# Attention and feed-forward in one kernel: two token blocks share each weight group, and the last tokens' value remainders take 128 rows

## The chip, the cores and the metric

The kernel runs on one core of one Trainium2 chip. The metric is the device time of one execution in microseconds (us); lower is better. Engines: PE (TensorE: matmuls; its weight loads are shown as PEld), DVE (VectorE), ACT (ScalarE), POOL (GpSimd) and SP (SyncE, which issues the DMAs here). All run side by side, and each takes its own instructions strictly in the order in which they stand in its program.

## The reference

Linear attention over 8 batches, 8 heads and 576 tokens of 64 values, then a feed-forward layer (512 to 2048 to 512) over the 4608 tokens, all in float32:

```
def phi(x):                                   # x: b h s 64, w_phi: 64 x 128
    proj = einsum('bhsd,df->bhsf', x, w_phi)
    proj = proj - max(abs(proj), axis=-1)
    return concatenate([exp(proj), exp(-proj)], axis=-1)
q_p, k_p = phi(q), phi(k)
kv  = einsum('bhsf,bhsd->bhfd', k_p, v)
den = einsum('bhsf,bhf->bhs', q_p, sum(k_p, axis=2))[..., None] + 1e-6
x   = (einsum('bhsf,bhfd->bhsd', q_p, kv) / den)     # tokens x 512
h   = x @ w_in
out = maximum(0.01 * h, h) @ w_out
```

## The kernel before

**Attention** works on 32 *pairs* (a batch and two of its heads; four pairs make a batch). `k_phase(i)` turns the keys and values of pair i into a 256 x 66 matrix; `q_phase(i)` projects the queries (L317 for pairs 4 to 7, L319 and L320 later), transposes, subtracts the maximum, transposes back into `mb` (L338), takes the exponentials, multiplies with the pair's matrix (L358), divides (L369 to L374) and leaves x in `ring`. `ring` has two halves, one for even and one for odd batches. Pairs 0 to 3 go a quicker way at the start: `first_k_phase`, and `first_q_phase` in three units of 256, 256 and 64 tokens, so that unit 0 makes the x of token block 0 and unit 1 that of block 1. Pairs below 8 (`nat`) use plain float32 matmuls; from pair 8 on each operand is split in a rounded part and a remainder (names ending in h and l), and the product takes three matmuls.

**The feed-forward layer** works on 18 blocks of 256 tokens and 16 groups of 128 hidden values. One *step* (i, ft) is `layer1` (12 matmuls of 256 columns into the PSUM tile `h`, then `g` on ACT, `gh` on ACT, `gl` on POOL) and `layer2` (6 matmuls of 512 columns into two PSUM tiles `acc`). `split(i)` cuts a block's x in `xh` and `xl`. The blocks come one after the other.

**The weights** arrive in 32 *pieces* (`load_weights`: w_in and w_out for each of the 16 groups), as 64-bit words that are turned into float32 on the chip: two ACT operations, four DVE operations (L158, L159, L160, L163), a cast on ACT and a remainder on DVE (L72, `w0l` or `w1l`). The raw words of all pieces go through two places in the odd half of `ring` (`stage`). So no x of batch 1 can be written there until the last piece has been read.

**What sets the order**: the program is written with priorities (weights and attention ahead of the feed-forward steps), and a scheduler lays every instruction into its engine's fixed order at build time. `advance` and `room` say how far attention may run ahead. PSUM has eight banks: three `a` (attention's projections), one `c`, two `h`, two `acc`. Tiles with one tag share its buffers: a tile waits until an earlier holder of its buffer has been read for the last time.

**The last 64 tokens** of a pair (512 to 575) are kept for both heads in one tile, `kst`: rows 64 to 127 hold the rounded part, rows 0 to 63 the remainder. Their value remainders `vl` stand in rows 64 to 127 alone, so that the product L266 runs over 64 rows; L267, beside it, runs over 128.

Of the kernel before, what the change touches and what calls it, by code (L numbers as in the profile page):

```python
# [44 lines left out]
def attention_moe_kernel(ctx: ExitStack, tc: tile.TileContext, q, k, v, vt, w_phi, w_in, w_out, out):  # L45
# [5 lines left out]
    def ct(shape, dt, name):  # L51
        return cp.tile(shape, dt, tag=name, name=name)
# [39 lines left out]
    wq = ct([P, 2, F], F32R, "wq")  # L92
    wq_h, wq_l = wq[:, 0], wq[:, 1]
    bd = ct([P, 2 * F], F32, "bd")
    vh = ct([P, 10, 66], F32R, "vh")
    vl = ct([P, 10, 64], F32R, "vl")
    nc.gpsimd.memset(vh[:, :, 64:66].bitcast(F32), 1.0)

    f1, f2, f3, f4 = (cp.tile([P, 2048], F32, tag="late", name=n, bufs=4) for n in ("f1", "f2", "f3", "f4"))
    fk = [None, f2, f1, f4]  # L100
# [41 lines left out]
            nc.scalar.copy(wq_h[r], w)  # L142
            nc.vector.tensor_tensor(wq_l[r], w, wq_h[r].bitcast(F32), op=ALU.subtract)

    stage = ring[:, 1].rearrange("p a s -> p (a s)")

    def load_weights():
        n = 0
        for ft in range(NFT):
            for which, src in ((0, w_in), (1, w_out)):  # L150
                raw = stage[:, 1024 * (n % 2) : 1024 * (n % 2) + 1024].bitcast(I32)
                nc.sync.dma_start(raw, src[:, ft].bitcast(I32))
                raw = raw.rearrange("p (n t) -> p n t", t=2)
                low, top = raw[:, :, 0], raw[:, :, 1]
                w = st([P, DM], F32, "ql")
                wi = w.bitcast(I32)
                nc.scalar.activation(w, top.bitcast(F32), AF.Abs)
# [21 lines left out]
        kraw[i] = rk, rv  # L179

    def load_q(i):
        rq = st([P, S], F32, "qs" if i < NN and i % 2 else "rq")
        nc.sync.dma_start(rq, q[i])
        qraw[i] = rq

# [2 lines left out]
    def k_phase(i):  # L188
        nat = i < NK
        rk, rv = kraw.pop(i)  # L190
        if not nat:
            ks = st([P, 2, S], F32R, "ks")
            for j in range(2):
                o, n = slice(64 * j, 64 * j + 64), slice(64 - 64 * j, 128 - 64 * j)
                copy_("kh", ks[o, j], rk[o])
                nc.vector.tensor_tensor(ks[n, j], rk[o], ks[o, j].bitcast(F32), op=ALU.subtract)
            copy_("vh", vh[:, :, 0:64], rv[:, :, 0:64])
            for r, c in ((slice(0, P), slice(0, 8)), (slice(64, P), slice(8, 10))):
                tt_("vl", vl[r, c], rv[r, c, 0:64], vh[r, c, 0:64].bitcast(F32), ALU.subtract)
# [9 lines left out]
        for g in range(3):  # L209
            w = 2 if g < 2 else 1  # L210
            r = slice(0, P) if g < 2 else slice(64, P)
            n = P if g < 2 else 64
            m4 = st([P, 4], F32, "m4")
            pmk = st([P, 4, F], F32, "pmk")
            if nat:
                pk = pt("a")
                for s in range(w):
                    t0 = (2 * g + s) * P if g < 2 else S - P
                    proj(pk, s, rk[:, t0 : t0 + P])
                pkv = pk[r, 0 : 256 * w].rearrange("p (a f) -> p a f", f=F)  # L220
            else:
                for s in range(w):
                    t0 = (2 * g + s) * P if g < 2 else S - P
                    pk = pt("a")
                    for j in range(2):
                        nc.tensor.matmul(pk[:, 256 * j : 256 * j + 256], lhsT=ks[:, j, t0 : t0 + P],
                                         rhs=wq.rearrange("p a f -> p (a f)"), start=True, stop=True)
# [12 lines left out]
            yield  # L240
            for s in range(w):
                c = 2 * g + s
                ek = st([P, 2, 256], F32, ("ek", "kph", "kpl")[c % 3] if nat else "ek")
                nc.scalar.activation(ek[r, :, 0:F], pmk[r, 2 * s : 2 * s + 2], AF.Exp)  # L244
                nc.scalar.activation(ek[r, :, F:256], pmk[r, 2 * s : 2 * s + 2], AF.Exp, scale=-1.0)
                if nat:
                    for j in range(2):
                        kv_mm(j, rv[r, 4 * j + c if c < 4 else 8 + j], ek[r, j], first=c == 0, last=c == 4)
                    yield
                    continue  # L250
                if c < 4:
                    kph = st([P, 2, 256], F32R, "kph")
                    kpl = st([P, 2, 256], F32R, "kpl")
                    copy_("kph", kph, ek)
                    tt_("kpl", kpl, ek, kph.bitcast(F32), ALU.subtract)
                    for j in range(2):
                        kv_mm(j, vh[:, 4 * j + c], kph[:, j], first=c == 0)
                        kv_mm(j, vl[:, 4 * j + c], kph[:, j])
                    for j in range(2):
                        kv_mm(j, vh[:, 4 * j + c], kpl[:, j])  # L260
                else:
                    kst = st([P, 2, 256], F32R, "kph")
                    copy_("kst", kst[r], ek[r])
                    nc.vector.tensor_tensor(kst[0:64], ek[r], kst[r].bitcast(F32), op=ALU.subtract)
                    for j in range(2):
                        kv_mm(j, vl[r, 8 + j], kst[r, j])  # L266
                        kv_mm(j, vh[:, 8 + j], kst[:, j], last=True)  # L267
                yield
        kvs = st([P, 2, 256], F32, "ek").rearrange("p a (b f) -> p a b f", b=2)[0:66]
# [254 lines left out]
    accs = {}  # L524
    gs = {}

    def split(i):
        for d in range(NP):
            t0 = 0
            while t0 < T:  # L530
                c = (i * T + t0) % (2 * S)
                n = min(T - t0, S - c % S)
                x = ring[:, c // S, d, c % S : c % S + n]
                t1 = t0 + n
                copy_("xh", xh[:, d, t0:t1], x)
                tt_("xl", xl[:, d, t0:t1], x, xh[:, d, t0:t1].bitcast(F32), ALU.subtract)
                t0 = t1

    def layer1(i, ft):
        ph = pt("h")[:, 0:T]  # L540
        for d in range(NP):
            nc.tensor.matmul(ph, lhsT=weight(0, "h", ft)[:, d * P : d * P + P], rhs=xh[:, d], start=d == 0, stop=False)  # L542
            nc.tensor.matmul(ph, lhsT=weight(0, "l", ft)[:, d * P : d * P + P], rhs=xh[:, d], start=False, stop=False)  # L543
        for d in range(NP):
            nc.tensor.matmul(ph, lhsT=weight(0, "h", ft)[:, d * P : d * P + P], rhs=xl[:, d], start=False, stop=d == NP - 1)  # L545
        g = st([P, T], F32, "g")
        gh = st([P, T], F32R, "gh")
        gl = st([P, T], F32R, "gl")
# [34 lines left out]
    def room(i):  # L583
        return min(B, 2 + i * T // S) * NP
# [3 lines left out]
    together(first_k_phase(0), first_k_phase(1))  # L588
    together(first_k_phase(2), first_k_phase(3))
    together(first_q_phase(0))  # L590
    tc.cur_priority = PU
    first_load_q(1)
    first_load_q(2)
    together(first_q_phase(1))
    together(first_q_phase(2))
    split_w_phi()
    load_q(NP)
    tc.cur_priority = PW
    load_weights()
    tc.cur_priority = 0  # L600
    steps = [(i, ft) for i in range(NBLK) for ft in range(NFT)]
    split(0)
    for n, (i, ft) in enumerate(steps):
        layer1(i, ft)
        advance(min(room(i + 1), NP * (1 + (i + (ft + 1) / NFT) * T / S) + 2))
        if ft == NFT - 1 and i + 1 < NBLK:
            advance(math.ceil((i + 2) * T / S) * NP)
            split(i + 1)
        if n >= LAG:
            layer2(*steps[n - LAG])  # L610
# [39 lines left out]
```

## Time and profile before

| | |
|---|---|
| median of 3 runs | 1243.11 us (1240.61 to 1243.74) |
| the profiled execution | 1238.5 us, its span 1236.7 us |
| PE busy | 1187.8 us, 96% of the span |
| DVE, ACT, POOL busy | 854.6, 797.0, 669.4 us |
| mean granted TensorE clock | 0.994 |
| DMA | 57.00 MB, mean 46 GB/s |

A row of the timeline gives the start in us from the span's start, the duration, the engine, the line, and what is written and read. A row of the windows gives, for a stretch, each engine's busy time with the number of its instructions. PE's busy time can hide waiting, since matmuls overlap and their ends are modelled; the distance from one matmul's start to the next, and the number of matmuls in a stretch, tell more. A float32 matmul is recorded as two instructions.

### The profile page before, as it was taken

To read this page: it belongs to the slowest core of one execution; us is meant where nothing else is said; L and a number is where in the kernel's file an instruction comes from. 1 tells how busy PE (TensorE), PEld (TensorE's weight loads), DVE (VectorE), ACT (ScalarE), POOL (GpSimd) and SP (SyncE) were. 2 spreads that over 40 slices of the span, in tenths; PEclk is the share of its full clock that TensorE was granted. 3 is DMA by queue.
4 is the path that set the end of the run, shared out by engine and by line. 5 is a ranking of instruction groups with operands and counts; after the bars stand their busy time and mean duration, and the time that the engine had idled before them with its cause. 6 is when DMAs were issued, how large, how long until landed. Compare 5 with 4: busy or idle time off the path is not lost. (4 is left out here: it accounts for less than half of the span.)

```text
span 1236.7 us, 21143 instructions
## 1 busy us (share of the span) xinstructions
PE 1187.8 (96%) x7496; PEld 1035.8 (84%) x7496; DVE 854.6 (69%) x1357; ACT 797.0 (64%) x2027; POOL 669.4 (54%) x701
## 2 busy tenths in 40 slices
PE   8898799999999999999899999999999999999998
PEld 5686577779888989889798988989888888999997
DVE  6999854698888888888888898806887788200000
ACT  5987765677777777777677777736766766433232
POOL 0132122467767676767667777836666767433232
PEclk9999899999999999999999999999999999999999
DMA  7345411011111111111111111100111100000000
GB/s 209 116 135 160 147 47 41 10 54 34 39 30 48 31 35 44 31 48 31 30 38 39 31 48 31 39 20 28 31 48 31 29 20 1 19 17 1 18 18 17
DMA packets 62777, 57.00 MB, mean 46 GB/s; under 512 B 45136, under 2 KB 46288, under 8 KB 62672
## 3 DMA queue, kind: packets, MB, share of 16 engines
q1 hardware_dynamic: 62672, 55.65, 15.8%
q8 instruction: 59, 0.97, 0.3%
q14 instruction: 46, 0.38, 0.1%
HBM read 46.20 MB, written 9.44 MB: 45 GB/s over the span
## 5 line engine op out<-in xcount | busy, mean ns | idle before, releaser
L72 POOL TENSOR_TENSOR gl<-g,gh 128x256 fp32r<-128x256 f32 x288 | 241.9, 842 | 294.8 <-ACT gh L67 237.1
L542 PE MATMUL h<-xh,w0h 128*128 128x256 f32 x1152 | 299.1, 286 | 4.5 <-ACT g L549 1.8
L543 PE MATMUL h<-xh,w0l 128*128 128x256 f32 x1152 | 298.2, 285 | 0.4 <-DVE w0l L72 0.4
L562 PE MATMUL acc<-w1h,gh 128*128 128x512 f32 x576 | 231.0, 401 | 10.4 <-ACT gh L67 8.3
L542 PEld LDWEIGHTS h<-xh,w0h 128*128 128x128 f32 x1152 | 218.4, 190 | 21.2 <-ACT g L549 2.7
L543 PEld LDWEIGHTS h<-xh,w0l 128*128 128x128 f32 x1152 | 218.2, 189 | 14.3 <-issue 1.9
L563 PE MATMUL acc<-w1l,gh 128*128 128x512 f32 x576 | 228.5, 397 | 0.0
L564 PE MATMUL acc<-w1h,gl 128*128 128x512 f32 x576 | 220.3, 398 | 0.0
L545 PE MATMUL h<-xl,w0h 128*128 128x256 f32 x1152 | 206.3, 284 | 0.0
L549 ACT ACTIVATE g<-h 128x256 f32<-128x256 f32 x288 | 109.2, 382 | 133.3 <-PE h L545 93.6
L72 POOL TENSOR_TENSOR ql<-eq,qh 128x576 fp32r<-128x576 f32 x96 | 159.5, 1668 | 38.7 <-DVE qh L69 26.3
L545 PEld LDWEIGHTS h<-xl,w0h 128*128 128x128 f32 x1152 | 167.2, 190 | 2.1 <-issue 0.4
L67 ACT CAST gh<-g 128x256 fp32r<-128x256 f32 x288 | 114.3, 402 | 75.5 <-PE acc L563 72.3
L562 PEld LDWEIGHTS acc<-w1h,gh 128*128 128x128 f32 x576 | 109.0, 189 | 26.3 <-ACT gh L67 10.5
L72 POOL TENSOR_TENSOR kpl<-ek,kph 128x512 fp32r<-128x512 f32 x72 | 101.9, 1415 | 49.9 <-PE c L206 22.1
L69 DVE CAST qh<-eq 128x576 fp32r<-128x576 f32 x96 | 99.2, 1037 | 35.5 <-ACT eq L344 20.1
L564 PEld LDWEIGHTS acc<-w1h,gl 128*128 128x128 f32 x576 | 106.6, 189 | 19.5 <-POOL gl L72 0.5
L563 PEld LDWEIGHTS acc<-w1l,gh 128*128 128x128 f32 x576 | 109.1, 189 | 12.4
L69 DVE COPY o<-acc 128x512 f32<-128x512 f32 x17 | 11.7, 687 | 130.4 <-DMA out_dram<-o 129.5
L72 POOL TENSOR_TENSOR ring<-ring,mb 128x576 f32<-128x576 f32 (+1 forms) x37 | 47.9, 1293 | 88.2 <-DVE mb L500 42.9
L343 ACT ACTIVATE eq<-mb 128x288 f32<-128x288 f32 x112 | 49.3, 440 | 67.8 <-DVE mb L338 60.4
L244 ACT ACTIVATE ek<-pmk 128x256 f32<-128x256 f32 (+1 forms) x128 | 53.4, 417 | 58.6 <-POOL pmk L72 21.0
(176 smaller groups left out, 2412.3 us busy)
## 6 DMA issues: line engine op xcount, KB each, us to landing
out_dram<-o SPq DMA_DIRECT2D x35, 256.0 KB, 2.0
ring<-in_w_in_dram SPq DMA_DIRECT2D x16, 512.0 KB, 3.7
ring<-in_w_out_dram SPq DMA_DIRECT2D x16, 512.0 KB, 3.6
rk<-in_k_dram SPq DMA_DIRECT2D x27, 288.0 KB, 2.8
rq<-in_q_dram SPq DMA_DIRECT2D x26, 288.0 KB, 2.8
rv<-in_v_dram SPq DMA_DIRECT2D x29, 256.0 KB, 3.4
rv<-in_vt_dram SPq DMA_DIRECT2D x58, 32.0 KB, 2.9
f<-in_k_dram SPq DMA_DIRECT2D x3, 288.0 KB, 3.3
```

Source lines behind the costliest of these rows:

```text
L67: nc.scalar.copy(o, i)
L69: (nc.vector if e == "v" else nc.gpsimd).tensor_copy(o, i)
L72: (nc.vector if pick(key) == "v" else nc.gpsimd).tensor_tensor(o, a, b, op=op)
L244: nc.scalar.activation(ek[r, :, 0:F], pmk[r, 2 * s : 2 * s + 2], AF.Exp)
L343: nc.scalar.activation(eq[:, 0], mb[:, u], AF.Exp)
L542: nc.tensor.matmul(ph, lhsT=weight(0, "h", ft)[:, d * P : d * P + P], rhs=xh[:, d], start=d == 0, stop=False)
L543: nc.tensor.matmul(ph, lhsT=weight(0, "l", ft)[:, d * P : d * P + P], rhs=xh[:, d], start=False, stop=False)
L545: nc.tensor.matmul(ph, lhsT=weight(0, "h", ft)[:, d * P : d * P + P], rhs=xl[:, d], start=False, stop=d == NP - 1)
L549: nc.scalar.activation(g, ph, AF.Prelu, alpha=0.01)
L562: nc.tensor.matmul(a, lhsT=gh[:, ts], rhs=weight(1, "h", ft), start=ft == 0, stop=False)
L563: nc.tensor.matmul(a, lhsT=gh[:, ts], rhs=weight(1, "l", ft), start=False, stop=False)
L564: nc.tensor.matmul(a, lhsT=gl[:, ts], rhs=weight(1, "h", ft), start=False, stop=ft == NFT - 1)
```

## The change

1. **Blocks 0 and 1 take each weight group together.** The first 32 steps are (0,0), (1,0), (0,1), (1,1) and so on; block 1's x is split right after `first_q_phase(1)`. Its rounded part sits in the two buffers of `qh` (which pairs from 8 on need), its remainder in a tile `vx`, which is handed to the value tile `vhl` (the former `vh` and `vl`) once block 1 is through layer 1. Block 1's two output sums take one bank of `h` and one of `a`, so that one `h` and two `a` are left until both blocks are done.
2. **Raw words go elsewhere.** Pieces 0 to 9 go through the odd half of `ring`, 10 to 23 through the tiles `f4` and `f1` of the quick start (the second half of `f4` holds the matrix of pair 2 until unit 2 of the first queries has used it), and 24 to 31 through the second half of `ring`'s odd half (the places of pairs 6 and 7) and a buffer of `qs`. So x of pairs 4 and 5 may be written from piece 10 on, and x of pairs 6 and 7 after piece 30. The queries of pairs 5 and 7 no longer have a buffer of their own.
3. **128 rows.** Rows 0 to 63 of the last tokens' value remainders are set to zero once, and their product runs over all 128 rows. It now also waits for the remainder that DVE writes into rows 0 to 63 of `kst`.

```
+    xbh = [st([P, 2, U], F32R, "qh")[:, :, 0:T] for _ in range(2)]
+    xbl = cp.tile([P, NP, T], F32R, tag="vx", name="xbl", bufs=1)
...
+    def values():
+        if not split_v:
+            split_v[0] = vhl = cp.tile([P, 10, 130], F32R, tag="vx", name="vhl", bufs=1)
+            nc.gpsimd.memset(vhl[:, :, 64:66].bitcast(F32), 1.0)
+            nc.gpsimd.memset(vhl[0:64, 8:10, 66:130].bitcast(F32), 0.0)
+        return split_v[0][:, :, 0:66], split_v[0][:, :, 66:130]
...
-                raw = stage[:, 1024 * (n % 2) : 1024 * (n % 2) + 1024].bitcast(I32)
+                if n < 10:
+                    raw = ring[:, 1, 2 * (n % 2) : 2 * (n % 2) + 2].rearrange("p a s -> p (a s)")[:, 0:1024]
+                elif n < 24:
+                    raw = (f4[:, 0:1024], f4[:, 1024:2048], f1[:, 0:1024])[n % 3]
+                else:
+                    raw = st([P, 2 * S], F32, "qs")[:, 0:1024] if n % 2 else tail_stage[:, 0:1024]
...
-        rq = st([P, S], F32, "qs" if i < NN and i % 2 else "rq")
+        rq = st([P, S], F32, "rq")
...
-                        kv_mm(j, vl[r, 8 + j], kst[r, j])
+                        kv_mm(j, vl[:, 8 + j], kst[:, j])
...
+    split(0)
...
+    split(1, *xb)
...
+    for t in range(TT):
+        accs[1, t] = pt(('h', 'a')[t])
+        nc.vector.memset(accs[1, t][:, 0:1], 0.0)
+        accs[0, t] = pt("acc")
...
-    steps = [(i, ft) for i in range(NBLK) for ft in range(NFT)]
-    split(0)
+    steps = [(i, ft) for ft in range(NFT) for i in range(2)]
+    steps += [(i, ft) for i in range(2, NBLK) for ft in range(NFT)]
     for n, (i, ft) in enumerate(steps):
-        layer1(i, ft)
-        advance(min(room(i + 1), NP * (1 + (i + (ft + 1) / NFT) * T / S) + 2))
-        if ft == NFT - 1 and i + 1 < NBLK:
+        if i == 1:
+            layer1(i, ft, *xb)
+        else:
+            layer1(i, ft)
+        advance(min(room(0 if n < 2 * NFT - 1 else i + 1), NP * (1 + (n + 1) / NFT * T / S) + 2))
+        if i and ft == NFT - 1 and i + 1 < NBLK:
```

Three places show how the instructions move; the line numbers are those of each kernel's own file (the changed file's L396, L508, L562, L563, L565 and L582 to L584 are L378, L490, L542, L543, L545 and L562 to L564 before; its L175 to L180 are L158 to L163, its L335 is L317 and its L376 is L358). On PE, this is the last pair of unit 1 of the first queries (`c<-qs`) and unit 2 behind it (`128x64`), with the steps around them. Before:

```order
L490 MATMUL c<-qs,f_79 128x256 x2
L564 MATMUL acc<-w1h_718,gl 128x512 x2
L542 MATMUL h<-xh,w0h_705 128x256
L317 MATMUL a<-rq,bd 128x288
L543 MATMUL h<-xh,w0l_706 128x256
```

Steps of block 0 alone surround it. After:

```order
L508 MATMUL c<-qs,f_82 128x256 x2
L396 MATMUL a<-bd,ks 128x256 x2
L562 MATMUL h<-qh,w0h_638 128x256
L563 MATMUL h<-qh,w0l_639 128x256
L508 MATMUL c<-eq,f_81 128x64 x2
```

Before, block 0's steps with later groups (`w0h_705` is the second tile of four groups) stand around them; now it is the first step of block 1 (`qh` is its x), which needs the x of all four pairs, and the next step of block 0 stands behind it.

On DVE, this is where piece 10 of the weights (its L158, now L175) comes. Before, pieces go on all the while between the divisions of the first queries (L497 to L500):

```order
L500 STREAM_TRANSPOSE mb<-rc 128x256
L158 TENSOR_SCALAR ql<-ql 128x512
L163 ISA ql<-ql,kvl 128x1024
L234 TENSOR_REDUCE m_1007<-a 128x4
L159 TENSOR_SCALAR ql<-ql 128x512
```

Pieces and attention take turns there. After, all of the first queries and the keys of pair 4 and some of pair 5 stand ahead of it:

```order
L517 RECIPROCAL rc<-mb 128x8
L518 STREAM_TRANSPOSE mb<-rc 128x256
L255 TENSOR_TENSOR pmk<-a,m_1062 64x256
L175 TENSOR_SCALAR ql<-ql 128x512
L176 TENSOR_SCALAR ql<-ql 128x512
L177 SCALAR_TENSOR_TENSOR ql<-f_83,ql 128x512
```

Piece 10 (read from `f_83`, which is `f4`) now stands behind the last division of unit 2.

On PE again, this is where pair 6 multiplies with its matrix (`a<-eq,kvh`). Before, it stands in block 1, in the third group of weight tiles:

```order
L564 MATMUL acc<-w1h_718,gl 128x512
L542 MATMUL h<-xh,w0h_797 128x256
L358 MATMUL a<-eq,kvh 128x288 x2
L543 MATMUL h<-xh,w0l_798 128x256
L358 MATMUL a<-eq,kvh 128x288
```

They are woven one by one into a layer 1. After:

```order
L584 MATMUL a<-w1h_835,gl 128x512
L376 MATMUL a<-eq,kvh 128x288 x4
L294 MATMUL c<-ident,ek 128x66 x4
L562 MATMUL h<-qh,w0h_914 128x256
L563 MATMUL h<-qh,w0l_915 128x256
```

It stands in the fourth group (`w0h_914`) between steps of block 0 and block 1, and PE can take none of the rows behind it until its exponentials are there.

More of the change, by code (lines that the diff above doesn't have):

```diff
@@ L94, in attention_moe_kernel @@
     bd = ct([P, 2 * F], F32, "bd")
-    vh = ct([P, 10, 66], F32R, "vh")
-    vl = ct([P, 10, 64], F32R, "vl")
-    nc.gpsimd.memset(vh[:, :, 64:66].bitcast(F32), 1.0)
+    xbh = [st([P, 2, U], F32R, "qh")[:, :, 0:T] for _ in range(2)]
+    xbl = cp.tile([P, NP, T], F32R, tag="vx", name="xbl", bufs=1)
+    for x in xbh:
+        nc.gpsimd.memset(x[:, 0, 0:2].bitcast(F32), 0.0)
+    nc.gpsimd.memset(xbl[:, 0, 0:2].bitcast(F32), 0.0)
+    xb = [xbh[d // 2][:, d % 2] for d in range(NP)], [xbl[:, d] for d in range(NP)]
+    split_v = {}
+    def values():
[4 more added lines that the diff above has]
+        return split_v[0][:, :, 0:66], split_v[0][:, :, 66:130]
     f1, f2, f3, f4 = (cp.tile([P, 2048], F32, tag="late", name=n, bufs=4) for n in ("f1", "f2", "f3", "f4"))
@@ L143, in split_w_phi @@
             nc.vector.tensor_tensor(wq_l[r], w, wq_h[r].bitcast(F32), op=ALU.subtract)
-    stage = ring[:, 1].rearrange("p a s -> p (a s)")
+    tail_stage = ring[:, 1, 2:4].rearrange("p a s -> p (a s)")
     def load_weights():
@@ L150, in load_weights @@
             for which, src in ((0, w_in), (1, w_out)):
-                raw = stage[:, 1024 * (n % 2) : 1024 * (n % 2) + 1024].bitcast(I32)
+                if n < 10:
[4 more added lines that the diff above has]
+                    raw = st([P, 2 * S], F32, "qs")[:, 0:1024] if n % 2 else tail_stage[:, 0:1024]
+                raw = raw.bitcast(I32)
                 nc.sync.dma_start(raw, src[:, ft].bitcast(I32))
@@ L196, in k_phase @@
                 nc.vector.tensor_tensor(ks[n, j], rk[o], ks[o, j].bitcast(F32), op=ALU.subtract)
+            vh, vl = values()
             copy_("vh", vh[:, :, 0:64], rv[:, :, 0:64])
@@ L525, in attention_moe_kernel, with split @@
     gs = {}
-    def split(i):
+    x0 = [xh[:, d] for d in range(NP)], [xl[:, d] for d in range(NP)]
+    def split(i, xh=x0[0], xl=x0[1]):
         for d in range(NP):
@@ L534, in split, with layer1 @@
                 t1 = t0 + n
-                copy_("xh", xh[:, d, t0:t1], x)
-                tt_("xl", xl[:, d, t0:t1], x, xh[:, d, t0:t1].bitcast(F32), ALU.subtract)
+                copy_("xh", xh[d][:, t0:t1], x)
+                tt_("xl", xl[d][:, t0:t1], x, xh[d][:, t0:t1].bitcast(F32), ALU.subtract)
                 t0 = t1
-    def layer1(i, ft):
+    def layer1(i, ft, xh=x0[0], xl=x0[1]):
         ph = pt("h")[:, 0:T]
         for d in range(NP):
-            nc.tensor.matmul(ph, lhsT=weight(0, "h", ft)[:, d * P : d * P + P], rhs=xh[:, d], start=d == 0, stop=False)
-            nc.tensor.matmul(ph, lhsT=weight(0, "l", ft)[:, d * P : d * P + P], rhs=xh[:, d], start=False, stop=False)
+            nc.tensor.matmul(ph, lhsT=weight(0, "h", ft)[:, d * P : d * P + P], rhs=xh[d], start=d == 0, stop=False)
+            nc.tensor.matmul(ph, lhsT=weight(0, "l", ft)[:, d * P : d * P + P], rhs=xh[d], start=False, stop=False)
         for d in range(NP):
-            nc.tensor.matmul(ph, lhsT=weight(0, "h", ft)[:, d * P : d * P + P], rhs=xl[:, d], start=False, stop=d == NP - 1)
+            nc.tensor.matmul(ph, lhsT=weight(0, "h", ft)[:, d * P : d * P + P], rhs=xl[d], start=False, stop=d == NP - 1)
         g = st([P, T], F32, "g")
```

## The prediction

> **What bounds the kernel now.** I read the page's first lines, then the windows, then the timelines of PE and DVE over the first 260 us, and at last the groups by shape.
>
> ```profile
> span 1236.7 us, 21143 instructions
> ...
> PE 1187.8 (96%) x7496; PEld 1035.8 (84%) x7496; DVE 854.6 (69%) x1357; ACT 797.0 (64%) x2027; POOL 669.4 (54%) x701
> ```
>
> PE is the bound over the whole; the next engine is at 69%. Where PE falls short is read from the windows (busy us and number of instructions of each engine):
>
> ```profile
> 0.00:60.00 60.00, 51.48 (x235) 36.41 (x236) 47.62 (x92) 44.19 (x93) 4.66 (x17) 1.00 0.58 166
> 60.00:100.00 40.00, 37.47 (x216) 31.72 (x215) 38.26 (x73) 33.29 (x75) 12.44 (x15) 1.00 0.47 141
> 100.00:160.00 60.00, 48.57 (x233) 35.25 (x232) 52.11 (x96) 43.96 (x96) 8.42 (x12) 0.91 0.46 135
> 160.00:240.00 80.00, 80.00 (x449) 63.91 (x448) 44.14 (x83) 46.83 (x128) 29.05 (x38) 1.00 0.14 38
> 240.00:260.00 20.00, 16.33 (x82) 12.38 (x81) 15.18 (x31) 15.42 (x37) 6.49 (x10) 0.91 0.26 73
> 260.00:1060.00 800.00, 781.39 (x5204) 700.67 (x5203) 652.01 (x980) 557.11 (x1452) 550.88 (x533) 1.00 0.12 33
> 1060.00:1220.00 160.00, 160.00 (x1019) 144.83 (x1018) 4.61 (x7) 52.66 (x140) 53.78 (x76) 1.00 0.03 12
> ```
>
> From 1060 on there is no attention left and PE runs dense: 1019 matmuls in 160 us. In 100 to 160 it starts 233 in 60 us, in 240 to 260 it starts 82 in 20 us; DVE is busy 90.4 of the 100 us from 60 to 160 (38.26 + 52.11), then 44 of 80. So PE starves in the first 160 us, where DVE has the weights and attention together, and once more at 240. Afterwards it is nearly full.
>
> These rows of the timelines place four events: the last piece of the weights on DVE, pair 6's first transpose into `mb`, pair 7's last query projection on PE, and the first matmul of block 2 that waited for the x of pair 7.
>
> ```profile
> 161.70 0.67 DVE L72 TENSOR_TENSOR w1l<-ql,w1h 128x512 fp32r<-128x512 f32 x1
> ...
> 203.94 0.77 DVE L338 STREAM_TRANSPOSE mb<-tq 128x576 f32<-128x576 f32 x1
> ...
> 226.94 0.75 PE L317 MATMUL a<-qs,bd 64*128 64x288 f32 x2
> ...
> 255.09 0.39 PE L542 MATMUL h<-xh,w0h 128*128 128x256 f32 x1 [0.65 <-ACT xh L67]
> ```
>
> **Part 3 of the change, the 64-row matmuls.** The groups by shape, and two of these matmuls among their neighbours:
>
> ```profile
> L206 PE MATMUL c<-kph,vl 128*64 128x256 f32 x192 | 49.5, 280 | 0.0
> L206 PE MATMUL c<-kph,vl 64*64 64x256 f32 x48 | 15.7, 328 | 0.7 <-DVE kph L69 0.7
> L206 PEld LDWEIGHTS c<-kph,vl 128*64 128x64 f32 x192 | 25.8, 134 | 2.2
> L206 PEld LDWEIGHTS c<-kph,vl 64*64 64x64 f32 x48 | 6.2, 129 | 10.4 <-issue 5.4 <-DVE kph L69 1.6 <-DVE kph L264 0.6
> ```
>
> ```profile
> L264 DVE TENSOR_TENSOR kph<-ek,kph 64x512 fp32r<-64x512 f32 x24 | 18.9, 786 | 0.8
> ```
>
> ```profile
> 280.49 0.40 PE L564 MATMUL acc<-w1h,gl 128*128 128x512 f32 x1
> 280.73 0.28 PE L542 MATMUL h<-xh,w0h 128*128 128x256 f32 x1
> 280.84 0.28 PE L543 MATMUL h<-xh,w0l 128*128 128x256 f32 x1
> 281.05 0.33 PE L206 MATMUL c<-kph,vl 64*64 64x256 f32 x1
> 281.31 0.39 PE L542 MATMUL h<-xh,w0h 128*128 128x256 f32 x1
> 281.53 0.28 PE L543 MATMUL h<-xh,w0l 128*128 128x256 f32 x1
> 281.65 0.28 PE L542 MATMUL h<-xh,w0h 128*128 128x256 f32 x1
> ...
> 282.00 0.27 PE L206 MATMUL c<-kph,vh 128*66 128x256 f32 x1
> 282.20 0.33 PE L206 MATMUL c<-kph,vl 64*64 64x256 f32 x1
> 282.46 0.34 PE L206 MATMUL c<-kph,vh 128*66 128x256 f32 x1
> 282.63 0.40 PE L226 MATMUL a<-wq,ks 128*128 128x256 f32 x2
> ```
>
> A 256-column matmul normally starts 0.12 us after the one ahead (280.73 to 280.84, 281.53 to 281.65), and a 512-column one takes 0.23 (280.49 to 280.73 for 0.24). Around the 64-row one three distances are long: to it 0.21, from it 0.26, and from the next 0.22. That is 0.69 instead of 0.36, a loss of 0.33 us; at 282.20 it is 0.20, 0.26 and 0.17, a loss of 0.27. The weight load's idle time says the same: 10.4 us ahead of 48 loads of 64 rows, 2.2 ahead of 192 loads of 128 rows. PE evidently neither overlaps the load of a 64-row operand with the matmul ahead nor the next load with it. With 128 rows the matmul has the shape of the 192, which have no idle time ahead. Two per pair for pairs 8 to 31 are 48, times 0.30 us makes 14.4 us, up to 16 at 0.33. Below, nothing, if 128 rows bring the same stall; a loss is bounded by the new wait for DVE's remainder (L264 below), which L267 right beside it already has today, so I leave it out. PE is 98% busy from 260 to 1060 (781 of 800), where all but two of these matmuls lie; the 19 us of idle there end on other engines, and a matmul saved ahead of such a wait may only lengthen it. I take 13.
>
> A rule of the Trainium skill speaks against this term. Its page "TensorE: Matmul & The Clock Gate", section "Why this matters for your kernels", says that a single matmul over 32 rows takes as long as one over 128, so that few rows cost nothing by themselves; by it this term would be 0. The trace differs: 328 ns against 280 for the matmul itself, and 0.26 against 0.12 us to the next start. I go by the rows, and keep the rule as a rival.
>
> **Parts 1 and 2, the front.** I counted the work that stands ahead of an event in each engine's order: on PE 0.117 us for 256 columns, 0.23 for 512, 0.43 for a 256-column float32 matmul; on DVE each group's mean. Ahead of pair 7's last projection (226.94) stand 175.8 us of matmuls before (30 layer 1 and 27 layer 2 among them), and 175.8 after (29 and 28). So what the front gains is what PE loses less up to there; before, 226.94 - 175.8 = 51 us are lost. From that projection to the x of pair 7 it is a chain of DVE, ACT, PE and POOL, 255.09 - 226.94 = 28 us, which keeps its instructions.
>
> What PE loses after, in order:
>
> (a) Up to the first step 15 us as before, which are loads and the quick start. Then block 1's first step stands ahead of block 0's second. It needs the x of unit 1 of all four pairs, and these share one `c` bank. Without steps between, their products follow each other about 4 us apart, as the first two of these rows do:
>
> ```profile
> 66.69 1.13 PE L490 MATMUL c<-qs,f 128*128 128x256 f32 x4 [1.02 <-ACT dn L494]
> 70.44 1.02 PE L490 MATMUL c<-qs,f 128*128 128x256 f32 x4
> 77.14 1.02 PE L490 MATMUL c<-eq,f 128*128 128x256 f32 x4
> ...
> 91.99 1.02 PE L490 MATMUL c<-qs,f 128*128 128x256 f32 x4
> ...
> 97.00 1.89 PE L490 MATMUL c<-eq,f 128*128 128x64 f32 x16
> ```
>
> From 66.69 four more halves (two pairs) end near 82, and unit 2 near 85 instead of 99. Block 0's second step, with 65.7 us of matmuls ahead of it, then comes near 87: 21 us lost, against 18 at that point before. This is a loss of 3, counted in what follows.
>
> (b) Piece 10 goes to the second half of `f4`, free only after unit 2 (85). The load's landing, its first ACT operation, and one issue on SP before:
>
> ```profile
> ring<-in_w_in_dram SPq DMA_DIRECT2D x16, 512.0 KB, 3.7
> ...
> L157 ACT ACTIVATE ql<-ring 128x512 f32<-128x512 f32 x32 | 21.6, 675 | 15.1 <-DMA ring<-in_w_in_dram 6.9 <-DMA ring<-in_w_out_dram 5.1 <-DVE w0l L72 1.5
> ...
> 37.73 0.33 SPq L152 DMA_DIRECT2D ring<-in_w_out_dram  x1
> ```
>
> With 3.7 us for the load and 0.68 on ACT, DVE starts piece 10 near 90, with 76 us of its work done. Pieces 11, 12, 24 and 25 are issued earlier on SP but stand behind it on DVE. Piece 12's load stands ahead of piece 5's there, and waits until pair 3's keys have left `f4`, near 40; piece 5 was issued at 37.73, so it may come 2 us later, covered by the two pieces ahead of it on DVE. Loads of pairs 4 to 6 stand between the pieces and wait for buffers that attention has left by then: nothing.
>
> (c) From there to pair 6's transpose stand 186.6 - 76 = 110.6 us of DVE work at group means. DVE's early work is shorter than these means: by 160 us it was busy 138.0 us (47.62 + 38.26 + 52.11) for some 154 us so counted, 0.9. So 99 us, and 5 for waits within attention's chains: 90 + 104 = 194, against 204.7 before, though more of the weights stand ahead of the last attention pieces (the last piece has 176.6 us of DVE work ahead instead of 156.1). PE reaches that point with 161 us of matmuls; it will have waited there from about 185 on, since by the same counts the weights themselves are 15 to 25 us ahead of their steps. So DVE sets this point and no longer the missing weights.
>
> (d) From 194: 2 us to the first product, 4 to the second (one `mb`, two `eq`), then 11.7 us of matmuls to pair 7's last projection: 211, against 227 before. The front gains 16 us. The chain of 28 us behind it stands as it was, so the second hole at 240 to 260 remains and only comes earlier. Cover: in (d) the steps between fill PE; if ACT is late with `g`, the single `h` bank bares it (a rival below).
>
> Bounds of this term: above, PE never waits for attention after (a): 175.8 + 24 = 200, a gain of 27. Below, the nearest row is before's own 204.7 for the transpose (a gain of about 4, since the products follow sooner); and with the `h` bank as limit a loss. I take 16, nearest to the DVE sum.
>
> Two memsets on DVE and two on POOL, of few elements, and the copies of `split(1)`, which move but stay as many, cost nothing: ACT is busy 33 of 40 us and POOL 12 of 40 there. Behind step 34 the order of PE is almost the same in both kernels (within 6 us of matmuls everywhere), so the rest keeps its 42 us of other losses.
>
> **Sum.** 16 + 13 = 29 us off. The profiled execution has 1238.5 us, of which the span is 1236.7; 1238.5 - 29 = 1209.5. The median of the runs is 4.6 us above it: 1243.1 - 29 = 1214.
>
> **Rivals.** The measurement can't tell less than about 0.3% (3.7 us) from no change.
> - *The front gives nothing.* Attention's chain for pairs 6 and 7 is late whatever the weights do: x of pairs 6 and 7 may only be written after piece 30, which is later now. For it: 20.5 us more DVE work ahead of the last piece; against: DVE was idle 36 of 80 us from 160 on. It leaves 13 to 15: 1229.
> - *The front gives all.* PE never waits for DVE after (a): 27 + 14, 1202. For it: DVE's early work is shorter than I count; against: (b).
> - *Remainders cost the same in 128 rows* (the change then does not do what part 3 says): only the front is left, 1227. This is what the skill's rule makes of it.
> - *One `h` bank.* The next layer 1 waits until ACT has read the bank:
>
> ```profile
> L549 ACT ACTIVATE g<-h 128x256 f32<-128x256 f32 x288 | 109.2, 382 | 133.3 <-PE h L545 93.6 <-POOL gl L72 37.3
> ```
>
> Between two layer 1 stand 6 matmuls of 0.23, 1.4 us, which cover the 0.38. If ACT works on attention first (two exponentials and a cast are about 1.5 us), some 0.5 us would show per step, 16 us for 32; from 0.9 us on (29 / 32) the kernel is slower, and 1.3 us per step gives 1256. Against it: ACT is busy 83% from 60 to 100 only, and later less.
> - *Both terms fail*: 1243.
>
> **How the numbers follow.** Forecast 0.57 (1207 to 1221 by its own bounds: the front 10 to 21, the remainders 11 to 15), front nothing 0.16, front all 0.12, remainders nothing 0.07, both fail 0.04, one `h` bank 0.04. The range 1201 to 1231 takes in the first four and leaves out 0.1 to 0.15. Faster 0.92, same 0.04, slower 0.04.
>
> **What would show it.** Part 3: no 64-row group left of `vl`, its 48 matmuls near 280 ns, and distances of 0.12 us around them. (a): block 0's second step near 87. (b): piece 10 on DVE near 90. (c): pair 6's transpose near 194, with PE idle ahead of it on DVE or ACT. (d): pair 7's last projection near 211, and the first matmul that waits for its x near 239. If PE's idle time in the first 200 us is ended by `g`, the `h` bank was the limit; if the transpose comes after 204, the front was worth nothing.

## The result and the profile after

| | kernel before | kernel after |
|---|---|---|
| median of four runs each, us | 1242.97 (1240.61 to 1243.74) | 1231.02 (1229.39 to 1232.45) |
| ratio to before, 95% interval | | 0.9907 [0.9888, 0.9925] |
| profiled execution, span, us | 1236.7 | 1227.6 |

The change saves 12 us (9 to 14), where 29 were forecast. The time is just past the far end of the range of 1201 to 1231. The first lines of the page after are:

```profile
span 1227.6 us, 21133 instructions
...
PE 1179.4 (96%) x7496; PEld 1033.1 (84%) x7496; DVE 839.9 (68%) x1359; ACT 795.7 (65%) x2027; POOL 665.8 (54%) x705
```

The same windows as before (busy us and number of instructions of each engine) show where PE gained and where it did not:

```profile
0.00:60.00 60.00, 50.89 (x232) 35.86 (x232) 47.70 (x93) 44.22 (x93) 4.73 (x19) 1.00 0.64 183
60.00:100.00 40.00, 35.55 (x193) 27.27 (x192) 28.49 (x59) 29.88 (x73) 12.78 (x18) 1.00 0.32 90
100.00:160.00 60.00, 59.25 (x334) 47.21 (x333) 56.26 (x108) 47.41 (x108) 13.35 (x16) 1.00 0.44 127
160.00:240.00 80.00, 76.39 (x417) 60.70 (x417) 54.73 (x95) 55.35 (x141) 27.44 (x36) 0.98 0.23 67
240.00:260.00 20.00, 19.66 (x140) 18.07 (x139) 17.02 (x27) 13.09 (x35) 9.75 (x11) 1.00 0.13 32
260.00:1060.00 800.00, 774.14 (x5159) 696.75 (x5158) 632.97 (x976) 554.61 (x1446) 545.88 (x532) 1.00 0.12 33
```

By 260 us PE has started 1316 matmuls (232 + 193 + 334 + 417 + 140), 101 more than before. In the 800 us from there it starts 5159, 45 fewer than the 5204 before, although 48 of its matmuls have lost their stall. So the front gained, and the middle gave much of it back. The events that the prediction named came nearly when it said:

```profile
87.72 0.47 PE L562 MATMUL h<-xh,w0h 128*128 128x256 f32 x1
```

```profile
88.54 0.43 DVE L175 TENSOR_SCALAR ql<-ql 128x512 f32<-128x512 f32 x1 [0.97 <-ACT ql L174]
...
192.29 0.76 DVE L356 STREAM_TRANSPOSE mb<-tq 128x576 f32<-128x576 f32 x1
```

```profile
212.90 1.23 PE L335 MATMUL a<-rq,bd 64*128 64x288 f32 x4
...
239.08 0.41 PE L562 MATMUL h<-xh,w0h 128*128 128x256 f32 x1
```

These are block 0's second step (87 forecast), piece 10 of the weights on DVE (90), pair 6's transpose (194), pair 7's last projections (211; the row holds two, the second starts at 213.5) and block 2's first matmul (239). The groups of the remainders, by shape, show 128 rows in every one of them:

```profile
L224 PE MATMUL c<-kph,vhl 128*64 128x256 f32 x240 | 62.5, 283 | 0.3 <-DVE kph L282 0.2
...
L224 PEld LDWEIGHTS c<-kph,vhl 128*64 128x64 f32 x240 | 32.6, 136 | 4.2 <-DVE kph L282 1.5
```

So the question was where the middle lost it. In the text below, "lost" is the time from one matmul's start to the next beyond the usual distance of its kind, added up over a stretch. From 260 us on, before lost 51 us by this measure, after 63.5. Of the 51, 8 lie beside the 64-row matmuls, whose own long distance counts here as usual. So what the forecast called the 42 us of other losses has become 63.5.

### The profile page after: what moved, and what is told of

The parts are those of the page before. It is cut to its first block, busy times and chain, and to the rows that moved or that the text cites. A ratio compares the mean times of both kernels' runs of the same rounds, so it can differ in the third digit from the quotient of the medians.

```text
span 1227.6 us, 21133 instructions
## 1 busy us (share of the span) xinstructions
PE 1179.4 (96%) x7496; PEld 1033.1 (84%) x7496; DVE 839.9 (68%) x1359; ACT 795.7 (65%) x2027; POOL 665.8 (54%) x705
## 5 line engine op out<-in xcount | busy, mean ns | idle before, releaser
L562 PE MATMUL h<-xh,w0h 128*128 128x256 f32 x1088 | 278.4, 284 | 4.0 <-ACT xh L67 1.7
L563 PE MATMUL h<-xh,w0l 128*128 128x256 f32 x1088 | 276.3, 282 | 0.0
L562 PEld LDWEIGHTS h<-xh,w0h 128*128 128x128 f32 x1088 | 205.6, 189 | 16.1 <-ACT xh L67 2.3
L582 PE MATMUL acc<-w1h,gh 128*128 128x512 f32 x544 | 216.3, 398 | 2.2 <-DVE o L69 1.5
L583 PE MATMUL acc<-w1l,gh 128*128 128x512 f32 x544 | 214.8, 395 | 0.0
L563 PEld LDWEIGHTS h<-xh,w0l 128*128 128x128 f32 x1088 | 205.6, 189 | 8.6
L584 PE MATMUL acc<-w1h,gl 128*128 128x512 f32 x544 | 205.4, 396 | 1.2 <-POOL gl L72 1.2
L565 PE MATMUL h<-xl,w0h 128*128 128x256 f32 x1088 | 189.0, 283 | 0.3 <-POOL xl L72 0.2
L565 PEld LDWEIGHTS h<-xl,w0h 128*128 128x128 f32 x1088 | 155.3, 190 | 2.4 <-POOL xl L72 1.9
L584 PEld LDWEIGHTS acc<-w1h,gl 128*128 128x128 f32 x544 | 100.1, 188 | 19.6 <-POOL gl L72 2.2
L582 PEld LDWEIGHTS acc<-w1h,gh 128*128 128x128 f32 x544 | 102.5, 188 | 16.2 <-DVE o L69 2.5
L224 PE MATMUL c<-kph,vhl 128*66 128x256 f32 (+1 forms) x480 | 77.9, 284 | 6.1 <-ACT kph L67 3.3
```

What stands on the lines that cost most here:

```text
L224: nc.tensor.matmul(kvp[0 : lt.shape[1], 256 * j : 256 * j + 256], lhsT=lt, rhs=rt, start=first and j == 0, stop=last, skip_group_check=True)
L582: nc.tensor.matmul(a, lhsT=gh[:, ts], rhs=weight(1, "h", ft), start=ft == 0, stop=False)
L583: nc.tensor.matmul(a, lhsT=gh[:, ts], rhs=weight(1, "l", ft), start=False, stop=False)
L584: nc.tensor.matmul(a, lhsT=gl[:, ts], rhs=weight(1, "h", ft), start=False, stop=ft == NFT - 1)
```

## Experiments

The scheduler makes a new order for every edit: 128 rows alone move PE's instructions in some 300 places, and going back to 64 rows in the kernel after moves them in some 230. So some kernels below hold the order. Edges that set the order of issue, and add no wait, tie each engine's instructions to the order of the kernel named, and differ from it in nothing but the edit. Times are given by their ratio to before in 5 rounds; 0.001 is 1.24 us, and an interval is some 0.001 to 0.002 to either side, so that a difference of two rows of the tables is known to 2 or 3 us. The mean granted clock of the runs lies between 0.990 and 0.997. A difference of 0.001 in it is at most 1.2 us of PE's work, by estimate, and is named where it bears on a comparison.

### The third part in a fixed order and in its own

Theory D is that the 64-row stall is saved one for one in a fixed order; theory C is that PE waits for attention's chain and PE time saved turns into waits. The edit on the kernel before (on the kernel after, the last two lines are reversed):

```diff
+    nc.gpsimd.memset(vl[0:64, 8:10].bitcast(F32), 0.0)
...
-                        kv_mm(j, vl[r, 8 + j], kst[r, j])
+                        kv_mm(j, vl[:, 8 + j], kst[:, j])
```

> The kernel before with the third part alone: 128 rows instead of 64 for the last tokens' remainders (rows 0 to 63 of vl hold zeros), and every engine's instructions held in exactly the order of the kernel before. Theory D (the 0.3 us of a 64-row matmul is saved one for one as long as the order stays, and what the middle lost came from the new order): 1243 minus 12 to 14, about 1230. Theory C (from 260 us on PE waits for attention's chain on DVE, ACT and POOL, so that PE time saved there turns into waits in any order): 1238 to 1243, and PE's lost time from 260 to 1060 stays near 48 us.

> The kernel after with the third part undone (64 rows again), every engine held in exactly the order of the kernel after. Theory D: 1231 plus 12 to 14, about 1244, the same as before, since in this order nothing hides the 64-row matmuls. Theory C: 1231 to 1235, since the waits shrink by what the 64-row matmuls cost.

> The third part alone on the kernel before, in the order that the scheduler itself then makes (its order differs from before's in some 300 places on PE, all behind the first 10%). Theory D: 1230 plus or minus what such a reordering is worth; if this is several us from the same edit in before's order, the order alone has a price of that size. Theory C: 1238 to 1243 like the kernel in before's order.

> Parts one and two alone: the kernel after with 64 rows, in the order that the scheduler makes for it. The forecast's front gain of 16 us would give 1227 if the rest kept its losses as before. Theory D: between 1227 and 1244, set by how its new order happens to fall. Theory C: 1231 to 1235, because the rows don't matter there.

| kernel | median, us | ratio [95%] |
|---|---|---|
| before with 128 rows, before's order | 1238.8 | 0.9970 [0.9959, 0.9981] |
| before with 128 rows, own order | 1232.5 | 0.9921 [0.9908, 0.9933] |
| after with 64 rows, after's order | 1238.4 | 0.9966 [0.9954, 0.9978] |
| after with 64 rows, own order | 1249.3 | 1.0061 [1.0047, 1.0076] |

The first row lies where theory C put it, the second near where theory D did, and the last two where neither did.

The stall itself is as forecast. These are the four products with pair 9's last tokens (two remainders, two values, 256 columns) in the same place of the same order. With 64 rows:

```profile
279.06 0.39 PE L565 MATMUL h<-xl,w0h 128*128 128x256 f32 x2
279.38 1.11 PE L224 MATMUL c<-kph,vhl 64*64 64x256 f32 x4
280.33 0.29 PE L337 MATMUL a<-qs,wq 128*128 128x288 f32 x1
```

With 128:

```profile
276.39 0.40 PE L565 MATMUL h<-xl,w0h 128*128 128x256 f32 x2
276.62 0.64 PE L224 MATMUL c<-kph,vhl 128*64 128x256 f32 x4
277.10 0.30 PE L337 MATMUL a<-qs,wq 128*128 128x288 f32 x1
```

From the L565 row to the L337 row it is 1.27 us against 0.71, so 0.56 for the pair; the median of the 24 pairs is 0.57, which makes 13.7 us. (The mean is 0.53, 12.7 us, since a few pairs differ.) Of these the time of the kernel shows 0.9966 - 0.9907 = 0.0059, 7.3 us. The clock can have a part in that: its mean is 0.992 in the runs with 64 rows and 0.994 with 128, which is up to 2.5 us of the 7.3. In this fixed order the rest of the 13.7 should be waits. PE's list of waits from 260 to 1060 grows with 128 rows at the operands of attention, such as `qh` (3.6 to 4.3 us) and `kvl` (0.9 to 2.3), which is 2.1 us of it. Neither theory had 7.3: D asked for 12 to 14, C for 0 to 4.

In before's order the third part also brings a wait that the forecast left out. The scheduler had put other work between a pair's first remainder product and the value product that needs DVE's half of `kst`. With 64 rows only the second one waits for DVE; with 128 the first one does, and everything behind it. The same place before and with 128 rows:

```profile
907.27 0.33 PE L206 MATMUL c<-kph,vl 64*64 64x256 f32 x1
...
910.17 0.33 PE L206 MATMUL c<-kph,vh 128*66 128x256 f32 x1 [0.51 <-DVE kph L264]
```

```profile
908.37 0.38 PE L207 MATMUL c<-kph,vl 128*64 128x256 f32 x1 [2.87 <-DVE kph L265]
```

Over the middle this is, in that kernel's list of waits (us in total, times, longest):

```profile
PE c L207 <- DVE kph L265: 8.4, 8, 2.9
```

In the kernel after the scheduler has put the four products together behind DVE's half, and the group above has 0.2 us of this wait left. So the 8.4 us belong to the old order and not to the change, and 0.9970 is no measure of the stall.

The fourth row is the surprise: parts one and two alone, with a front that gains 15 us, are 7 us slower than before. In after's order the same instructions take 10.8 us less. So the third part is not what the middle lost.

### Extra PE work, and blocks 4 and 6 without their wait

In the kernel after, PE loses 10 us from 360 to 390 and 4 from 510 to 530; the two stretches lost 3 and 2 before. At 382 block 4 goes on, the first that needs the x of pair 11:

```profile
367.34 0.28 PE L563 MATMUL h<-xh,w0l 128*128 128x256 f32 x1
...
378.69 0.40 PE L337 MATMUL a<-qs,wq 128*128 128x288 f32 x1 [0.31 <-DVE tq L339]
378.93 0.29 PE L338 MATMUL a<-qs,wq 128*128 128x288 f32 x1
380.32 0.40 PE L337 MATMUL a<-qs,wq 128*128 128x288 f32 x1 [1.09 <-DVE tq L339]
...
381.87 0.39 PE L562 MATMUL h<-xh,w0h 128*128 128x256 f32 x1 [1.02 <-ACT xh L67]
```

By the first row all 64 steps of blocks 0 to 3 have had their layer 1, and the first two of block 4 have been begun with pairs 8 to 10, each in one of the two `h` banks; they wait for pair 11 until the last row. In between PE has a few layer 2 products and then only attention, and waits for its transposes. Before, when the last product of pair 11's queries came, 62 of the 64 steps had begun, so there was work in hand. That product came at about the same time in both kernels, before and after:

```profile
374.42 0.43 PE L363 MATMUL a<-ql,kvh 128*128 128x288 f32 x2
```

```profile
373.27 0.42 PE L381 MATMUL a<-ql,kvh 128*128 128x288 f32 x2
```

So the steps were ahead by what the front had gained, but attention was not (theory L, for lead). The rival was theory O: the losses are many small waits of the new order. Two edits tell them apart. One adds PE work, in held orders (here for the kernel after, without the lines that hold the order):

```diff
         ph = pt("h")[:, 0:T]
+        if i == PAD_BLOCK:
+            for _ in range(4):
+                nc.tensor.matmul(ph, lhsT=weight(0, "h", ft)[:, 0:P], rhs=xh[0], start=True, stop=True)
```

The other lets blocks 4 and 6 read other columns:

```diff
-                x = ring[:, c // S, d, c % S : c % S + n]
+                half = i * T % (2 * S) // S if i in (4, 6) else c // S
+                x = ring[:, half, d, c % S : c % S + n]
```

> The kernel before in its own order, with 4 more 256-column matmuls ahead of layer 1 in each of block 2's 16 steps (the first product once more, overwritten): 64 x 0.117 = 7.5 us of PE work between about 240 and 310 us. Theory L (lead: what counts in this stretch is how far the MLP steps stand behind the x that they need; before, PE reaches block 4, step 64, and block 6, step 96, after the x of pairs 11 and 15 is there, with 2 to 3 steps of work in hand, so PE is the bound): nearly all of it is paid, +6 to +8 us, 1248 to 1250. Theory O (order: PE's waits in the middle are many small ones that any PE time fills up, before as after): +2 to +5.

> The same 64 matmuls in block 2 of the kernel after, in after's own order. Theory L: after, PE has run out of MLP steps when it comes to block 4 (10 us lost from 360 to 390) and again at block 6, since the x of pair 11 comes at 373 us as before; work put in ahead of that fills the hole: +0 to +3 us, 1231 to 1234. Theory O: the same +2 to +5 as in the kernel before; if PE is the bound there, +7.

> The same 64 matmuls in block 9 of the kernel after, about 710 to 780 us, behind both of the holes. Theory L: from block 6 on attention is ahead and PE is the bound, so nearly all is paid: +5 to +8 us. Theory O: +2 to +5, as at block 2.

> The kernel after, where the last columns of blocks 4 and 6 are read from the batch ahead (their outputs are then those of other tokens), so that these two blocks no longer wait for the x of pairs 11 and 15; the work is the same, and the scheduler makes its own order, which differs from after's from about a fifth of PE's order on. (The same edit on the kernel before leaves its order the same on all engines: there nothing waited for these.) Theory L: the holes at 360 to 390 and 510 to 530 go, 5 to 10 us, 1221 to 1226. Theory O: within 3 us of after, either way.

| kernel | median, us | ratio [95%] | against the kernel it is made from |
|---|---|---|---|
| before, 7.5 us more PE work in block 2 | 1245.1 | 1.0029 [1.0020, 1.0038] | +3.6 us |
| after, the same in block 2 | 1234.0 | 0.9941 [0.9926, 0.9955] | +4.2 |
| after, the same in block 9 | 1231.4 | 0.9924 [0.9910, 0.9938] | +2.1 |
| after, blocks 4 and 6 without the wait | 1224.8 | 0.9861 [0.9844, 0.9878] | -5.7 |

Theory O had the first three rows and missed the last; theory L had the last and missed the first three. PE time is paid by about half wherever it is put, also where MLP steps (steps of the feed-forward layer) were at hand: 0.3 to 0.6 of itself, of which the 0.3 in block 9 is uncertain (2.1 us, known to some 3). Without their wait the two blocks give 5.7 us back. That kernel has an order of its own, and its mean clock is 0.997 against 0.994, which is up to some 4 us; after's clock was halved right behind both holes, as the last section shows. In the windows, before, after, and without the wait:

```profile
340.00:380.00 40.00, 38.08 (x250) 33.33 (x249) 32.82 (x52) 27.69 (x73) 23.98 (x24) 1.00 0.12 31
380.00:420.00 40.00, 39.20 (x268) 35.58 (x267) 36.59 (x57) 29.96 (x81) 30.81 (x34) 1.00 0.17 46
```

```profile
340.00:380.00 40.00, 35.07 (x218) 29.28 (x217) 31.50 (x50) 25.55 (x70) 25.60 (x28) 1.00 0.13 38
380.00:420.00 40.00, 37.80 (x245) 33.86 (x246) 29.74 (x48) 25.98 (x69) 23.75 (x23) 0.96 0.11 31
```

```profile
340.00:380.00 40.00, 38.10 (x249) 33.86 (x248) 30.44 (x45) 27.91 (x77) 26.94 (x31) 1.00 0.12 31
380.00:420.00 40.00, 39.45 (x267) 35.74 (x266) 33.47 (x54) 27.73 (x72) 26.96 (x25) 1.00 0.13 37
```

In these 80 us PE starts 518, 463 and 516 matmuls.

### Why attention was not earlier: the shared tile, and the order with it

Pair 7's x came 16 us earlier, as forecast, yet pair 11's only 1. Pair 8 is the first with split values, which ACT copies into `vh` (after: `vhl`). Before, the copy waits for its DMA; after, it stands right behind PE's last read of `xbl`, block 1's remainders, whose memory it takes (tag `vx`, one buffer):

```profile
209.68 0.73 ACT L67 CAST vh<-rv 128x640 fp32r<-128x640 f32 x1 [0.99 <-DMA rv<-in_vt_dram]
```

```profile
222.47 0.63 PE L565 MATMUL h<-xbl,w0h 128*128 128x256 f32 x4
```

```profile
223.14 0.73 ACT L67 CAST vhl<-rv 128x640 fp32r<-128x640 f32 x1
```

No wait shows at that row, since ACT has other work up to it. But the copy is 13.5 us later than before, in a front that is 16 us earlier. That the tile holds attention back is theory V. The edit gives `vhl` its own memory:

```diff
-    xbl = cp.tile([P, NP, T], F32R, tag="vx", name="xbl", bufs=1)
+    xbl = [ct([P, 2, T], F32R, "xbl"), st([P, DM], F32R, "o").rearrange("p (a t) -> p a t", t=T)]
...
-            split_v[0] = vhl = cp.tile([P, 10, 130], F32R, tag="vx", name="vhl", bufs=1)
+            split_v[0] = vhl = ct([P, 10, 130], F32R, "vhl")
...
-            dn = st([P, U], F32, "dn")[:, 0:w]
+            dn = st([P, 2, 2, U], F32, "tq")[:, 0, 0, 0:w]
```

> The kernel after, where pair 8's split values (vhl) have memory of their own instead of sharing the tile of block 1's remainders (xbl); xbl goes half to a new tile and half to the output tile o, and dn takes tq's place for room. The work is the same. Theory V (the shared tile: in the kernel after ACT's first copy into vhl starts at 223.14 us, just when block 1's last layer 1 has read xbl at 223.10, and in the kernel before at 209.7; so attention from pair 8 on gets none of the 16 us that the front gained, PE runs ahead of it and is out of MLP steps at blocks 4 and 6): the copy comes near 210, pair 11's x near 363 instead of 373, the loss from 360 to 390 goes from 10 to about 4, and the time is 4 to 10 us less, 1221 to 1227. Theory O (many small waits of the new order, no single cause): within 3 us of after.

> The same kernel with own memory for vhl, in exactly its order, but with 64 rows again for the last tokens' remainders (13.7 us of distances more). If the half of it that the kernel after kept (7.4 of 13.7) was a matter of the holes at blocks 4 and 6, then with these holes smaller more of it is paid: 10 to 13 us above the kernel it is made from. If waits for attention swallow half of any PE time in the middle, 6 to 8 us.

> Own memory for vhl, and blocks 4 and 6 read their last columns from the batch ahead (their outputs are then those of other tokens), so that they don't wait for the x of pairs 11 and 15. Theory V: the holes are already mostly filled, so this is worth 0 to 3 us more, where the same edit on the kernel after was worth 5.7. Theory O with holes that have another cause: 4 to 6 us more.

| kernel | median, us | ratio [95%] |
|---|---|---|
| own memory for `vhl` | 1219.7 | 0.9827 [0.9814, 0.9840] |
| the same order, 64 rows | 1222.8 | 0.9855 [0.9842, 0.9869] |
| own memory, blocks 4 and 6 without the wait | 1216.8 | 0.9802 [0.9788, 0.9816] |

With own memory the kernel takes 9.9 us less than the kernel after, a little more than theory V asked for, at the same mean clock (0.994). Its ACT copy, pair 11's last product, and its windows:

```profile
198.15 0.73 ACT L67 CAST vhl<-rv 128x640 fp32r<-128x640 f32 x1 [0.79 <-DMA rv<-in_vt_dram]
```

```profile
364.48 0.43 PE L382 MATMUL a<-ql,kvh 128*128 128x288 f32 x2
```

```profile
340.00:380.00 40.00, 39.23 (x267) 35.51 (x266) 34.52 (x57) 30.77 (x82) 30.64 (x34) 1.00 0.15 34
380.00:420.00 40.00, 38.77 (x267) 35.27 (x267) 34.43 (x56) 27.80 (x74) 26.60 (x24) 1.00 0.15 44
...
260.00:1060.00 800.00, 778.64 (x5247) 709.83 (x5246) 634.93 (x970) 555.92 (x1449) 553.08 (x534) 1.00 0.12 33
```

The copy comes 25 us earlier, the holes are filled (534 matmuls in the 80 us), pair 11 is 9 us earlier, and the middle starts 88 more matmuls than after. From 260 on about 50 us are lost, 13 less than after, and still more than the 42 that the forecast wanted kept.

How much of this is the tile's own wait is not shown. This kernel's order on PE differs from after's in some 135 places, and the order alone was worth 10.8 us above. Pair 8's last query products, in the kernel after and with own memory, say how far the copy moved them:

```profile
268.90 0.42 PE L381 MATMUL a<-ql,kvh 128*128 128x288 f32 x2
```

```profile
267.36 0.30 PE L382 MATMUL a<-ql,kvh 128*128 128x288 f32 x1
```

Before, that product came at 277.84. So in the kernel after pair 8 was still 9 us ahead of before, and pair 11, three pairs on, 1 us. The copy that is 25 us later moved the end of pair 8 by less than 2 us; pair 11's 9 us grew behind it. A run with own memory in after's order, which would part the tile from the order, is missing.

What the holes still cost with own memory is 3.1 us (0.0025, hardly more than the two intervals), against 5.7 with the shared tile. The two are not told apart, and the mean clock (0.997 against 0.994) could be all of the 3.1. With 64 rows, and so with parts one and two alone, this kernel stands 18.0 us below before. By the distances in its profiled execution, whose span is 15.9 us below before's, 13 us lie up to step 40 and 3 behind it. The third part is then worth only 3.5 us, less than either expectation of it. Here the clock works the other way: 0.997 with 64 rows and 0.994 with 128, so that up to 3.4 us more of the stall may have been saved than the time shows, and the second expectation (6 to 8) would be met.

### Attention's chain with less work on DVE

What was open was why so little of the 13.7 us is paid. In the kernel with own memory, order held, both reductions take half the values:

```diff
-                nc.vector.tensor_reduce(m4[r, 0 : 2 * w], pkv, ...)
+                nc.vector.tensor_reduce(m4[r, 0 : 2 * w], pkv if nat else pkv[:, :, 0:64], ...)
...
-            nc.vector.tensor_reduce(m[:, j], blocks(tq[:, j]), ...)
+            nc.vector.tensor_reduce(m[:, j], blocks(tq[:, j]) if nat else blocks(tq[:, j])[:, :, 0:16], ...)
```

> The kernel with own memory for vhl, in exactly its order, where for pairs 8 to 31 the maxima of keys and queries are taken over half of the values only (two DVE reductions of 735 ns, two of 683 and one of 416 per pair become about half as long: some 1.3 us less of DVE's 27 us per pair; the maxima and so the outputs change). Theory C (from 260 us on PE's waits are set by attention's chain, in which DVE is the busiest): 3 to 10 us less, 1210 to 1217. If the waits have little to do with DVE: within 2 us of 1219.7.

> The same with 64 rows again for the last tokens' remainders (13.7 us more of distances on PE), same order. Theory C: with the chain shorter, PE is nearer to being the bound, and more of the 13.7 is paid than the 3.2 us (1222.8 to 1219.7) with the chain as it was: 5 to 10 us above the run with 128 rows. If the share that is paid is a property of the order alone: again 3 to 4 us.

Measured: 1212.4 us with 128 rows (0.9766 [0.9747, 0.9785]), 1219.3 with 64 (0.9816 [0.9795, 0.9837]), both inside what theory C asked for. PE's work is untouched, yet the time falls by 0.0061, 7.6 us (of which the clock, 0.997 against 0.994, is at most some 3), and 128 rows against 64 are now worth 0.0050, 6.2 us instead of 3.5. PE's row for the middle:

```profile
260.00:1060.00 800.00, 781.00 (x5283) 714.16 (x5282) 617.47 (x970) 556.78 (x1454) 556.18 (x536) 1.00 0.12 33
```

It starts 36 matmuls more than with the whole maxima, in the same order, and DVE is busy 17 us less. So in the middle PE waits for a chain in which DVE has a part: theory C holds, by halves. The step from 3.5 to 6.2 is no larger than what the four intervals and the clock leave open, so that more is paid with a shorter chain is not shown; that less work on DVE shortens the kernel is.

## Why the prediction was wrong

- **Up to 260 us: right.** Every event came within 3 us of its forecast, and up to step 40 PE loses 47.5 us instead of 62.5, a gain of 15 where 16 was taken. Waits for ACT to read the `h` bank into `g` come to 2.0 us (0.3 before), not to 16. So the rivals "front nothing" and "one `h` bank" are out, though the first, with its 1229, and "remainders the same", with 1227, named times near the measured one: that is chance, since the front gained and the stall went.
- **"The rest keeps its 42 us of other losses": the step that failed.** These losses became 63.5 us. The step rested on an order of PE that is almost the same behind step 34. The order does not tell when attention comes: its lead over the kernel before shrank from 16 us at pair 7 to 9 at pair 8 and 1 at pair 11, and the MLP steps ran out at blocks 4 and 6. One cause is at hand: block 1's remainders live in the tile that pair 8's values need, until block 1's last layer 1. Own memory, with the order that the scheduler makes for it, gave 9.9 us back. How much of that is the tile's wait and how much the order stays open. The prediction went through the buffers that the weights' pieces wait for, and never asked when `vx` and the `qh` pair come free, and who waits for them.
- **The remainders' 13: the mechanism right, the size wrong.** The stall is 0.57 us a pair, 13.7 in all, where 14.4 was summed; the rule that few rows cost nothing by themselves (the Trainium skill, "TensorE: Matmul & The Clock Gate", "Why this matters for your kernels") speaks of a single matmul; here, among matmuls of 128 rows, 64 rows did cost, as the prediction held. But the kernel's time shows 7.3 of it, and 3.5 with own memory for `vhl`. The prediction wrote that a matmul saved ahead of a wait may only lengthen it, and took off 1.4 us for that. It is about half or more.
- **The wait for DVE's half of `kst`, left out:** 8.4 us in the old order. In the kernel after the scheduler avoided it by moving the products.
- **The sum.** With own memory, parts one and two make 18 and the third 3.5, which is 21.5 of the 29; the shared tile, with the order that goes with it, takes 9.9 of these, which leaves 11.6, the measured 12. Against the forecast, 9.9 us are the tile and its order, 9.5 the remainders (13 - 3.5), and parts one and two were 2 better than the 16 taken. (The forecast's own lower bounds, 10 and 11, give 1222 where it has 1221.) The shares hang on where one starts: in after's order the third part shows 7.3, and parts one and two 4.2.

What stays open is why parts one and two in the scheduler's own order are 10.8 us slower than in after's. That kernel loses 7 us more from 500 to 540 than before, at block 6, where half of the clock was also gone for 10 us; why its attention came later there was not tried.

## What to carry to other kernels

When a change lends memory to an early stage, find the instruction that frees it and the first one that needs it, and set their times side by side: an engine with other work shows no wait there, and the loss can turn up 150 us later on another engine. Where an engine is 98% busy but its work is woven into another stage's chain, as here, count a saving on it at a quarter to a half until a run with a little more work on it, order held, has given the rate. And test an edit in a held order beside its own: here the order alone was worth up to 10.8 us, nearly as much as the change. An edit that makes its own order, as the one for own memory did, measures both.

## What the runs showed of the hardware

The clock was halved in the middle of the kernel, though PE was idle there for no longer than 1.4 us at a time. Windows of 3.41 us of the kernel after, in pairs that follow each other (busy us and matmuls of PE first, granted clock third from the end):

```profile
379.29:382.70 3.41, 1.36 (x9) 1.13 (x10) 3.32 (x7) 1.66 (x5) 2.46 (x3) 1.00 0.20 77
382.70:386.11 3.41, 3.41 (x18) 3.29 (x17) 3.28 (x7) 1.84 (x4) 0.00 (x0) 0.50 0.00 0
515.83:519.24 3.41, 1.89 (x12) 1.39 (x12) 3.25 (x6) 0.79 (x3) 0.92 (x2) 1.00 0.20 77
519.24:522.65 3.41, 3.41 (x18) 3.41 (x17) 3.38 (x8) 2.55 (x5) 1.86 (x3) 0.50 0.00 0
```

After 1.36 and 1.89 us of work in a window, the next one ran at 0.50, though it was full; by estimate that adds up to 1.7 us, half a window, to each hole. The share of work does not settle it: in the kernel before, a window with 1.88 us and an idle stretch of 1.53 us was followed by one at the full clock.

```profile
327.14:330.55 3.41, 1.88 (x12) 1.35 (x11) 3.38 (x7) 1.91 (x6) 0.30 (x2) 1.00 0.01 2
330.55:333.96 3.41, 3.41 (x25) 3.23 (x26) 2.90 (x4) 1.52 (x5) 2.41 (x2) 1.00 0.20 77
```

So no threshold comes out of these traces. The Trainium skill ("TensorE: Matmul & The Clock Gate", "Part 1: The HAM clock gate (the "warmup" mystery)") gives the length of the window as 3413 ns and its two clocks, and the trace agrees. The Trainium skill's advice to allow no gaps over some 3 us ("TensorE: Matmul & The Clock Gate", "Why this matters for your kernels") is too mild for this trace, where idle stretches of at most 1.4 us came ahead of a halved clock.
